# One list for five engines: an in-kernel planner fixes every engine's order in a fused SSM-convolution and MLP block, with loads off the ScalarE queue and smaller evictions

## The chip, the cores and the metric

The kernel runs on one core of a Trainium2 chip. The core has five engines that each work through their own list of instructions in order and wait for one another by semaphores: TensorE (PE in the profile, with its weight loads as PEld), VectorE (DVE), ScalarE (ACT), GpSimd (POOL) and SyncE (SP, which here only issues DMAs). ACT and POOL can issue DMAs too. Matrix products land in PSUM, eight banks that are used here as a ring of four tiles of two banks each; a tile comes free when ACT or DVE has copied it out ("evicted" it) to SBUF.

The metric is the device time of one execution in microseconds (us). Before the change its median is 469.66 us over three runs (469.36 to 471.55).

## What is computed

The reference, cut to what matters (B = 1, S = 2048 tokens, D = 640, F = 1728, all bf16):

```python
def _A_ref(q, k, v, shift_k, ssm_k, ssm_D):
    k_shift = sum(k_pad[:, t:t + S, :] * shift_k[:, ks - 1 - t] for t in range(4))
    kv = k_shift * v
    kv_f = rfft2(pad(kv), axes=(1, 2))
    kf_f = rfft2(pad(ssm_k), axes=(1, 2)).transpose(1, 2, 0)
    y = irfft2(kv_f * kf_f)[:S].astype(bfloat16)
    return q * (y + kv * ssm_D)
def _B_ref(x, w1, w2, w3, w4):
    h = gelu(layernorm(x) @ w1)
    g0, g1, g2, g3 = (h quarter by quarter, shifted by +1, -1, +2, -2 tokens)
    x1 = x + concatenate([g0, g1, g2, g3]) @ w2
    return x1 + gelu(layernorm(x1) @ w3) @ w4
sa, ca, ga, sb, cb, gb = (silu(c) @ w_mod).reshape(6, 640)
h = layernorm(A_q) * (1 + ca) + sa
x = A_q + ga * _A_ref(h, A_k, A_v, A_shift_k, A_ssm_k, A_ssm_D)
h = layernorm(x) * (1 + cb) + sb
return x + gb * _B_ref(h, B_w1, B_w2, B_w3, B_w4)
```

So there are two halves: a long convolution over the tokens (done by Fourier transforms that are written as matrix products), and a token-shift MLP.

## The kernel before

**Tables.** The Fourier matrices are built on the chip: POOL makes index ramps (iota, L127), DVE turns them into angles (L128 to L131), ACT takes sines (L135, L138) into F1bd (32x32 blocks), Gs in the region RG, and Hs in RH; EA and EB follow on DVE (L169).

**Loads.** ACT's queue issues ssm_k in five pieces (L90), the shift filter (L91) and k in four pieces (L93). SP's queue issues v with a transpose on the way (L95), then everything later: w_mod, x (A_q, L289), the MLP's weights, the transposes inside the MLP, and the output.

**Convolution.** "Slots" are 32x32 block transposes on DVE (L196) that bring time into the partitions. stage1 (L200) multiplies by F1bd, four matmuls to a PSUM tile of 1024 columns; stage2 (L210) multiplies by Gs, three frequencies to a tile, so 960 columns and eleven tiles for each of its two halves. Both run twice: for the kernel ssm_k (result KSX in R3) and for the signal kv (result XS in R5). Between the two come the shift filter (k is transposed on PE, evicted by ACT at L240, multiplied by diagonal matrices at L245, and multiplied by v on DVE at L248) and the six pieces of the modulation (L265). inverse1 (L350) multiplies the spectra on DVE (L358, L359; the second factor KSY is KSX with its halves swapped by DMA, in two buffers), and multiplies by EA and EB on PE; its evictions are all ACT's. inverse2 (L377) ends the convolution for two or three token tiles at a time. Evictions alternate between ACT and DVE by the patterns "AD" and "AAD" (make_evac, L181).

**MLP.** It runs in eight groups g of 256 tokens (two tiles A of 128): make_q (L328, layernorm of A_q, with 1-column steps on POOL for each tile), chain_a, chain_b, chain_c (residual, second layernorm, third layernorm; each with a square sum on ACT at L322 and a six-step finish on POOL, L313 to L318), a DMA transpose (L431), w1 (L439, L443), gelu on ACT, w2 (L492), another layernorm and DMA transpose (L501, L502), w3 (L513), gelu, w4 (L527), three DVE steps (L532 to L534) and the output DMA. The loop at L545 interleaves group g's chains and w1 with w2 of g-1 and w3, w4 of g-2.

**What sets the order.** The code is written stage by stage, and the framework's scheduler puts each engine's instructions into an order of its own when the program is built. DMAs of one queue are issued in order.

**Names that the prediction uses.** stage1, stage2, inverse1, inverse2 and the MLP's w1 to w4 as above; T01 holds stage1's result, later inverse1's, later the weights w3 and w4; Rb holds w_mod, later the products of inverse1, later y; "x" is A_q in Ra.

Of the kernel before, what the change touches and what calls it, by code (L numbers as in the profile page):

```python
# [16 lines left out]
P = 128  # L17
# [8 lines left out]

@with_exitstack
def kernel(
# [14 lines left out]
    psA = ctx.enter_context(tc.tile_pool(name="psA", bufs=4, space=PSUM))  # L43

# [5 lines left out]
    R5 = mem.tile([P, 20640], BF, name="R5")  # L50
    RG = mem.tile([P, 8192], BF, name="RG")
    RH = mem.tile([P, 4096], BF, name="RH")
    RK = mem.tile([P, 2048], BF, name="RK")
# [5 lines left out]
    ident = mem.tile([P, P], BF, name="ident")  # L59
    cga, sga, cb1, sbv, gbv = (modv[:, j, :] for j in range(5))  # L60
    T0, T1 = T01[:, 0:10240], T01[:, 10240:20480]
# [7 lines left out]
    vT = R5[:, 10400:20640].rearrange("p (b n) -> p b n", b=ND)  # L69
# [10 lines left out]
    KSY = [Rb[:, 8192:10240], RK[:]]  # L80
    y_all = Rb[:].rearrange("p (a d) -> p a d", d=D)

# [4 lines left out]
    with nc.allow_non_contiguous_dma(reason="tiny"):  # L87
        nc.scalar.dma_start(Dcol[:], A_ssm_D.rearrange("(b p) -> p b", p=P))
    for b in range(ND):
        nc.scalar.dma_start(sT[:, b, :], A_ssm_k[b * P:(b + 1) * P, :])  # L90
    nc.scalar.dma_start(skT[:], A_shift_k.rearrange("(b p) j -> p b j", p=P))  # L91
    for sc in range(4):
        nc.scalar.dma_start(ktok[:, 4 * sc:4 * sc + 4, :], k_flat[512 * sc:512 * sc + 512, :].rearrange("(t p) d -> p t d", p=P))  # L93
    for sc in range(4):
        nc.sync.dma_start_transpose(vT[:, :, sc * 512:(sc + 1) * 512], v_flat[sc * 512:(sc + 1) * 512, :])  # L95
    with nc.allow_non_contiguous_dma(reason="tiny"):
        nc.sync.dma_start(c_col[:], c.rearrange("o (b p) -> p (o b)", p=P))


    make_identity(nc, ident[:])  # L100
    mhalf = mem.tile([P, 4], F32, name="mhalf")
    nc.vector.memset(mhalf[:], -0.5)
    pidx = mem.tile([P, 1], I32, name="pidx")
    nc.gpsimd.iota(pidx[:], pattern=[[0, 1]], base=0, channel_multiplier=1)
    b_pos = mem.tile([P, 1], F32, name="b_pos")
    b_neg = mem.tile([P, 1], F32, name="b_neg")
    nc.vector.memset(b_pos[:], PI_LO)
    nc.vector.memset(b_neg[:], -PI_LO)
    T1i = T1.bitcast(I32)
    T1f = T1.bitcast(F32)  # L110
    ang_no = [0]

    def pcol(modulus, mult, add):
        ti = small.tile([P, 1], I32, name="pcol_i", tag="pcol_i")
        nc.vector.tensor_single_scalar(ti[:], pidx[:], modulus - 1, ALU.bitwise_and)
        tf = small.tile([P, 1], F32, name="pcol_f", tag="pcol_f", bufs=4)
        if mult != 1 or add != 0:
            nc.vector.tensor_scalar(tf[:], ti[:], float(mult), float(add), ALU.mult, ALU.add)
        else:
            nc.vector.tensor_copy(tf[:], ti[:])  # L120
        return tf

    def angles(s_col, n, pattern, base, q):
        o = 1536 * (ang_no[0] % 3)
        ang_no[0] += 1
        ti, ms, ma = (T1i[:, o + 512 * i:o + 512 * i + n] for i in range(3))
        nc.gpsimd.iota(ti, pattern=pattern, base=base, channel_multiplier=0)  # L127
        nc.vector.tensor_scalar(ms, ti, s_col, None, ALU.mult)  # L128
        nc.vector.tensor_single_scalar(ms, ms, q - 1, ALU.bitwise_and)
        nc.vector.tensor_scalar(ma, ti, s_col, float(q // 4), ALU.mult, ALU.add)  # L130
        nc.vector.tensor_single_scalar(ma, ma, q - 1, ALU.bitwise_and)  # L131
        return ms, ma

    def sin_to(dst, ms, q):
        nc.scalar.activation(dst, ms, ACT.Sin, scale=-2.0 * PI_LO / q, bias=b_pos[dst.start_partition():dst.start_partition() + dst.shape[0], :])  # L135

    def nsin_to(dst, ms, q):
        nc.scalar.activation(dst, ms, ACT.Sin, scale=2.0 * PI_LO / q, bias=b_neg[dst.start_partition():dst.start_partition() + dst.shape[0], :])  # L138

    cos_to = sin_to  # L140

    s32 = pcol(32, 1, 0)
    s32o = pcol(32, 2, 1)
    s64 = pcol(64, 1, 0)
    nc.gpsimd.memset(F1bd[:], 0.0)
    ms, ma = angles(s32[:], 32, [[2, 32]], 1, 128)
    for q in range(4):
        sl = slice(32 * q, 32 * q + 32)
        cos_to(F1bd[sl, q, 0, :], ma[sl, :], 128)
        nsin_to(F1bd[sl, q, 1, :], ms[sl, :], 128)  # L150
    for kb in range(4):
        ms, ma = angles(s64[:], 512, [[2, 8], [128, 64]], 1 + 16 * kb, 8192)
        k2s = slice(8 * kb, 8 * kb + 8)
        ms3, ma3 = (t.rearrange("p (a b) -> p a b", a=8) for t in (ms, ma))
        cos_to(Gs[:, k2s, 0, 0, :], ma3, 8192)
        nsin_to(Gs[:, k2s, 0, 1, :], ms3, 8192)
        sin_to(Gs[:, k2s, 1, 0, :], ms3, 8192)
        nc.gpsimd.tensor_copy(Gs[:, k2s, 1, 1, :], Gs[:, k2s, 0, 0, :])
    nc.gpsimd.affine_select(out=RQ[:, 0:2560].rearrange("p (a m) -> p a m", m=P),
# [7 lines left out]
    for E, i, src, sg in ((EA, 0, cs, (sc_, -sc_)), (EA, 1, sn, (sc_, -sc_)), (EB, 0, sn, (-sc_, -sc_)), (EB, 1, cs, (sc_, sc_))):  # L167
        for o in range(2):
            nc.vector.tensor_scalar_mul(E[64 * o:64 * o + 64, i, :], src[64 * o:64 * o + 64, :], sg[o])  # L169
# [58 lines left out]
    for b in range(ND):  # L228
        for h in range(2):
            stage1(sL, b, h, ev)  # L230
# [368 lines left out]
```

## Time and profile before

| what | value |
|---|---|
| median of three runs | 469.66 us |
| profiled execution | 471.74 us |
| its span, first to last instruction | 470.0 us |
| busy: PE, DVE, ACT, POOL | 308.2, 251.3, 228.6, 81.8 us |
| instructions | 7694 |
| mean granted TensorE clock | 0.855 |
| DMA traffic | 35.07 MB |

The profiled execution lies 2.08 us above the median, and 1.74 us of it are outside the span. No engine is busy all the time: PE has the most work, 66% of the span. A view by stretches gives each engine's busy time between two moments; a row of the timeline begins with its start and its duration; a row of the groups ends with "busy, mean ns of one | idle time before it, and what ended it".

### The profile page before, as it was taken

What the parts mean: (1) busy time and instruction counts of PE and PEld (TensorE: products, weight loads), DVE (VectorE), ACT (ScalarE), POOL (GpSimd) and SP (SyncE); (2) the same over time, 40 slices, a digit from 0 to 9 for tenths busy, and PEclk for the clock granted to TensorE, in tenths of its full rate; (3) what the DMA queues carried; (4) which work ended last, traced back from release to release, by engine and by line L of the source; (5) the groups of instructions that cost most, each with busy time, mean ns of one, the idle gap of its engine ahead of it and who ended that gap; (6) DMA issues with size and microseconds to landing.
All of it is one profiled execution on the core that took longest, in us unless ns stands there. A gap on an engine that the chain in (4) does not pass through costs nothing. (4 is left out here: it accounts for less than half of the span.)

```text
span 470.0 us, 7694 instructions
## 1 busy us (share of the span) xinstructions
PE 308.2 (66%) x3089; PEld 223.8 (48%) x3092; DVE 251.3 (53%) x441; ACT 228.6 (49%) x326; POOL 81.8 (17%) x238
## 2 busy tenths in 40 slices
PE   0031887676876508632720497996969889799995
PEld 0021643464556407521510374764747566477773
DVE  4967743984697779577777616133241522314113
ACT  0098724674499626664554271452716436251430
POOL 1331000000000250044544221120211202111000
PEclk9995899959997758965775599898979989899998
DMA  8950700014358507301671111012130111211211
GB/s 244 268 158 1 211 0 1 0 46 141 116 108 195 152 3 178 91 4 28 145 263 29 28 29 40 18 28 57 29 57 11 34 42 29 56 29 28 30 29 29
DMA packets 51219, 35.07 MB, mean 75 GB/s; under 512 B 35632, under 2 KB 48624, under 8 KB 51184
## 3 DMA queue, kind: packets, MB, share of 16 engines
q1 hardware_dynamic: 47040, 29.34, 26.4%
q10 hardware_dynamic: 4144, 5.25, 3.6%
q8 instruction: 24, 0.39, 0.3%
q14 instruction: 11, 0.09, 0.1%
HBM read 18.85 MB, written 2.62 MB: 46 GB/s over the span
## 5 line engine op out<-in xcount | busy, mean ns | idle before, releaser
L527 PE MATMUL ps_w<-T,R 128*128 128x320 bf16 x448 | 69.0, 300 | 0.8 <-ACT R L515 0.6
L439 PE MATMUL ps_w<-R,RG 128*128 128x256 bf16 x160 | 31.8, 386 | 56.2 <-DMA R<-RK 56.2
L513 PE MATMUL ps_w<-R,T 128*128 128x256 bf16 (+1 forms) x560 | 64.4, 273 | 0.0
L513 PEld LDWEIGHTS <-T 128*128 128x128 bf16 (+1 forms) x560 | 54.5, 99 | 8.2 <-issue 1.7
L527 PEld LDWEIGHTS <-R 128*128 128x128 bf16 x448 | 40.6, 97 | 29.0 <-issue 7.5
L439 PEld LDWEIGHTS <-RG 128*128 128x128 bf16 x160 | 21.1, 135 | 65.3 <-issue 55.3
L188 ACT CAST R<-ps_s 128x960 bf16<-128x960 f32 (+1 forms) x30 | 42.5, 1590 | 9.4 <-PE ps_s L218 9.4
L322 ACT ACTIVATE RG<-R 128x640 bf16<-128x640 bf16 x32 | 23.6, 736 | 45.7 <-DVE R L495 22.9
L207 PE MATMUL ps_s<-F1bd,Rb 128*128 128x256 bf16 x80 | 13.6, 342 | 41.7 <-ACT F1bd L138 27.4
L218 PE MATMUL ps_s<-T,RG 64*128 64x160 bf16 x512 | 28.9, 274 | 15.7 <-ACT R L188 7.3
L495 DVE SCALAR_TENSOR_TENSOR R<-ps_w,R 128x640 bf16<-128x640 f32 x16 | 13.1, 824 | 42.9 <-PE ps_w L492 42.8
L366 PE MATMUL ps_i<-EB,Rb 128*128 128x128 bf16 x160 | 22.2, 242 | 19.8 <-DVE Rb L359 19.8
L218 PEld LDWEIGHTS <-RG 64*128 64x128 bf16 x512 | 24.8, 114 | 19.9 <-issue 19.8
L532 DVE TENSOR_TENSOR T<-ps_w,R 128x640 bf16<-128x640 f32 x16 | 13.1, 820 | 39.4 <-PE ps_w L527 39.4
L440 ACT ACTIVATE R<-ps_w 128x1024 bf16<-128x1024 f32 x8 | 8.2, 1022 | 52.8 <-PE ps_w L439 52.8
L336 POOL TENSOR_SCALAR ln_rs<-ln_mv 128x1 f32<-128x1 f32 x16 | 4.7, 298 | 163.5 <-DVE ln_mv L333 143.7
L421 DVE TENSOR_SCALAR R<-Ra,ln_rs,ln_nb 128x640 bf16<-128x640 bf16 x16 | 6.4, 445 | 48.0 <-POOL ln_nb L318 48.0
L207 PEld LDWEIGHTS <-Rb 128*128 128x128 bf16 x80 | 9.6, 121 | 45.4 <-issue 42.4
L515 ACT ACTIVATE R<-ps_w 128x1024 bf16<-128x1024 f32 x24 | 23.6, 1021 | 12.6 <-PE ps_w L513 12.4
L340 ACT ACTIVATE RQ<-Ra,ln_nb,ln_rs 128x640 bf16<-128x640 bf16 x16 | 14.5, 918 | 29.2 <-POOL ln_nb L338 28.2
L492 PE MATMUL ps_w<-RG,R 128*128 128x320 bf16 x160 | 25.4, 301 | 3.8 <-ACT R L440 1.7
L366 PEld LDWEIGHTS <-Rb 128*128 128x128 bf16 x160 | 17.1, 110 | 21.2 <-DVE Rb L359 21.0
(110 smaller groups left out, 594.2 us busy)
## 6 DMA issues: line engine op xcount, KB each, us to landing
Rb<-in_w_mod_dram SPq DMA_DIRECT2D x6, 800.0 KB, 4.7
Ra<-in_A_ssm_k_dram ACTq DMA_DIRECT2D x5, 512.0 KB, 7.1
R<-in_A_k_dram ACTq DMA_DIRECT2D x4, 640.0 KB, 7.9
RK<-R SPq DMA_DIRECT2D x10, 256.0 KB, 3.7
Rb<-R SPq DMA_DIRECT2D x10, 256.0 KB, 3.5
Ra<-in_A_q_dram SPq DMA_DIRECT2D x4, 640.0 KB, 10.6
out_dram<-RH SPq DMA_DIRECT2D x64, 40.0 KB, 1.6
T<-in_B_w_dram SPq DMA_DIRECT2D x1, 2160.0 KB, 9.5
```

Source lines behind the costliest of these rows:

```text
L188: nc.scalar.copy(dst, src)
L207: nc.tensor.matmul(psv[:, ml, :], lhsT=xL[:, s0:s0 + P], rhs=F1r, start=True, stop=True)
L218: nc.tensor.matmul(psv[:, g, kl, :], lhsT=Gs[64 * g:64 * g + 64, k0 + kl, cc, :, :].rearrange("p o n -> p (o n)"), rhs=T1h[h][64 * g:64 * ...
L322: nc.scalar.activation(junk, src, ACT.Square, scale=float(D) ** -0.5, accum_out=stat[:, li, 1, t:t + 1])
L340: nc.scalar.activation(qt, xt, ACT.Identity, scale=rs[:], bias=nb[:])
L366: nc.tensor.matmul(psv[:, w, :], lhsT=TB[:, o:o + P], rhs=EBf, start=False, stop=True)
L439: nc.tensor.matmul(ps[:, fb, :], lhsT=w1_sb[:, b, 160 * fb:160 * fb + P], rhs=hT[:, b, :], start=(b == 0), stop=(b == ND - 1))
L492: nc.tensor.matmul(ps[:, hf, 0:320], lhsT=gsf[:, fb, c0:c0 + P], rhs=w2_sb[:, fb, 320 * hf:320 * hf + 320], start=(fb == 0), stop=(fb == 4))
L495: nc.vector.scalar_tensor_tensor(hv, ps[:, :, 0:320], 1.0, hv, ALU.mult, ALU.add, accum_out=stat[:, 2, 0, 2 * g + i:2 * g + i + 1])
L513: nc.tensor.matmul(ps[:fw, fl, :], lhsT=w3_sb[:, b, fb * P:fb * P + fw], rhs=xT[:, b, :], start=(b == 0), stop=(b == ND - 1))
L515: nc.scalar.activation(g3[g % 2][:, f0:f0 + fn, :], ps[:, 0:fn, :], ACT.Gelu_apprx_tanh)
L527: nc.tensor.matmul(ps[:, hf, 0:320], lhsT=g3[g % 2][:fw, fb, i * P:(i + 1) * P], rhs=w4_sb[:fw, fb, 320 * hf:320 * hf + 320], start=(fb == ...
```

## The change

The kernel's statements are wrapped into tasks. Each task has an engine (or a choice between ACT and DVE), an assumed cost, what it reads and writes, a priority, and the PSUM tile that it takes or frees. A planner inside the kernel (Planner.run) places them one after the other on five imagined clocks and sorts them by their planned start; they are then emitted in that order under manual_schedule, which leaves each engine's order as written. The planner runs while the program is built; the chip sees only the order.

What else is different:

- ssm_k pieces 0 and 1 go to SP's queue, pieces 2 to 4, the shift filter and k to POOL's queue. ACT issues no DMA.
- Angles: one ramp serves four tables, its offset is added on DVE by a column (gcol, hcol). The copies on POOL (L158) become four more sines on ACT.
- stage2 takes two frequencies to a tile: 640 columns, 16 tiles for each half, instead of 960 and eleven. Which engine evicts is the planner's choice, for the second half of the signal it is ACT's alone.
- The shift filter goes pair of feature blocks by pair of feature blocks ("b-major") over all tokens, in twelve units, interleaved with stage2 of the kernel. So the block transposes (slots) of kv can begin when a pair of blocks is done.
- KSY has three buffers instead of two.
- The layernorm of A_q: statistics of 16 tiles into one array, its finish on POOL for 6, 4 and 6 tiles at a time.
- All six pieces of inverse2 stand ahead of the first w1, with all evictions on ACT; the loads of w3 and w4 follow them on SP's queue.
- chain_c has four buffers instead of three.

```diff
+class Planner:
+    def run(self):
+        ...
+        while todo:
+            best = None
+            for e in engs:
+                cand = None
+                for t in ready[e]:
+                    ...
+                    st = max(rt, free[e])
+                    k = (st, t.prio) if st > free[e] else (free[e], t.prio)
+                    ...
+                if cand is not None and (best is None or cand[2] < best[2]):
+                    best = (cand[0], cand[1], cand[2], e)
+            ...
+        order.sort(key=lambda t: (t.start, t.no))
+        return order
...
     for b in range(ND):
-        nc.scalar.dma_start(sT[:, b, :], A_ssm_k[b * P:(b + 1) * P, :])
+        add("SP" if b < 2 else "POOL", 1.5 if b < 2 else 1.0, lambda e, b=b: (nc.sync if b < 2 else nc.gpsimd).dma_start(sT[:, b, :], ...),
...
-        nc.scalar.dma_start(ktok[:, 4 * sc:4 * sc + 4, :], ...)
+        add("POOL", 1.0, lambda e, sc=sc: nc.gpsimd.dma_start(ktok[:, 4 * sc:4 * sc + 4, :], ...),
...
-    def stage2(XSd, h, evac):
-        for k0 in range(0, 32, 3):
-            kn = min(3, 32 - k0)
+    def stage2(XSd, dreg, h, prio0, step=0.0, eng=("ACT", "DVE")):
+        for k0 in range(0, 32, 2):
...
+    units = [(sc, bp) for bp in ((0, 1), (2, 3), (4,)) for sc in range(4)]
...
+    for j in range(12):
+        k_transpose(j, 20 + (j - 2) / 3.0)
+    for j in range(12):
+        k_shift(j, 20 + j / 3.0)
     for h in range(2):
-        stage2(KSX, h, ev)
+        stage2(KSX, "R3", h, 20 + 2 * h, 1.0 / 16)
...
     for h in range(2):
-        stage2(XS, h, ev)
+        stage2(XS, "R5", h, 50, eng="ACT" if h else ("ACT", "DVE"))
...
+    for A in range(6):
+        ln1_stats(A, 66)
+    ln1_fin(0, 6, 66)
     for h in range(2):
         for b in range(ND):
-            inverse1(h, b, ev)
-            if h == 1:
-                make_q(b)
+            inverse1(h, b, 55 if h == 0 else 57)
+    for A in range(5):
+        make_q(A, 67)
...
+    for i, tl in enumerate(rest):
+        inverse2(tl, 105 + 5 * i)
...
+    dma("SP", 2200, w3t[0], w=[("T01", 0, ND * F)], prio=101)
+    dma("SP", 2200, w3t[1], w=[("T01", 10240, 10240 + NF * D, "w4")], prio=101)
...
+    order = pl.run()
...
+    with tc.manual_schedule():
+        for t in order:
+            t.fn(t.on)
```

Three places show what the order becomes.

ACT, the start of the program, before (the loads of ssm_k, of the filter and of k, then the first sines):

```order
L88 DMA Dcol<-in_A_ssm_D_dram 128x5x1
L90 DMA Ra<-in_A_ssm_k_dram 128x2048 x5
L91 DMA skT<-in_A_shift_k_dram 128x5x4
L93 DMA R_67<-in_A_k_dram 128x4x640 x4
L135 ACT_TABLE_LOAD
L135 ACTIVATE F1bd<-T_66,b_pos 32x32
```

ACT, the same place with the change:

```order
L331 ACT_TABLE_LOAD
L331 ACTIVATE F1bd<-R_67,b_neg 32x32 x2
L331 ACTIVATE F1bd<-R_67,b_pos 32x32 x3
L331 ACTIVATE F1bd<-R_67,b_neg 32x32
L331 ACTIVATE F1bd<-R_67,b_pos 32x32
```

The eleven DMA issues are gone from ACT, and the first sine stands at the head of its list.

DVE, where the signal's stage2 ends and inverse1 begins, before (L190 are evictions of stage2, L358 and L359 the products of inverse1, L332 and L333 the layernorm statistics of x):

```order
L190 CAST R_68<-ps_s_1249 128x320x3
L358 TENSOR_TENSOR Rb<-R_68,R_67 128x4x16x32
L359 TENSOR_TENSOR Rb<-R_68,RK 128x4x16x32
L190 CAST R_68<-ps_s_1291 128x320x3
L190 CAST R_68<-ps_s_1333 128x320x3
L358 TENSOR_TENSOR Rb<-R_68,R_67 128x4x16x32 x2
L332 BN_STATS ln_st<-Ra 128x6 x3
L333 BN_AGGR ln_mv<-ln_st 128x2
```

DVE, the same place with the change (L569 and L570 are the statistics, of which the last of eight tiles is shown, L520 to L524 the last pieces of the modulation, L608 and L610 the products, L588 and L589 the finish of a q tile):

```order
L569 BN_STATS ln_st<-Ra 128x6 x2
L570 BN_AGGR mv_93<-ln_st 128x2
L520 TENSOR_SCALAR modv<-ps_mod 128x640
L608 TENSOR_TENSOR Rb<-R_68,R_67 128x4x16x32
L522 CAST modv<-ps_mod 128x640
L524 CAST modv<-ps_mod 128x640
L608 TENSOR_TENSOR Rb<-R_68,R_67 128x4x16x32
L610 TENSOR_TENSOR Rb<-R_68,RK 128x4x16x32
L588 TENSOR_TENSOR RQ<-RQ,modv 128x640
L589 TENSOR_TENSOR RQ<-RQ,modv 128x640
L610 TENSOR_TENSOR Rb<-R_68,Rb 128x4x16x32
```

The statistics of eight tiles of x now stand ahead of the first product; before, four first products and two second ones stood ahead of them, and the other fourteen products behind.

SP, around the first transposes of the MLP, before (L354 and L355 are the swaps KSY, L431 the transposes after chain_c, L551 to L553 the loads of w3 and w4, L502 the transposes ahead of w3):

```order
L354 DMA RK<-R_67 64x2048
L355 DMA RK<-R_67 64x2048
L431 DMA_TRANSPOSE R_67<-RK 128x5x128 x4
L553 DMA T_66<-in_B_w_dram 64x640
L551 DMA T_66<-in_B_w_dram 128x5x1728
L552 DMA T_66<-in_B_w_dram 128x13x640
L502 DMA_TRANSPOSE R_67<-RH 128x5x128 x2
```

SP, the same place with the change (L603 the swaps, L900 to L902 w3 and w4, L734 the transposes after chain_c, L839 those ahead of w3):

```order
L603 DMA Rb<-R_67 64x2048 x2
L900 DMA T_66<-in_B_w_dram 128x5x1728
L901 DMA T_66<-in_B_w_dram 128x13x640
L902 DMA T_66<-in_B_w_dram 64x640
L734 DMA_TRANSPOSE R_67<-RK 128x5x128 x6
L839 DMA_TRANSPOSE R_67<-RH 128x5x128 x2
```

The two large loads moved from behind the transposes of the first two groups to ahead of them.

More of the change, by code (lines that the diff above doesn't have):

```diff
@@ L43 @@
     psA = ctx.enter_context(tc.tile_pool(name="psA", bufs=4, space=PSUM))
+    pl = Planner(4)
+    add = pl.add
+    eng_of = {"ACT": nc.scalar, "DVE": nc.vector}
     Ra = mem.tile([P, 10240], BF, name="Ra")
@@ L111 @@
[L111 to L146, printed above, removed]
+    stat = mem.tile([P, 3, 2, NT], F32, name="stat")
@@ L267 @@
[L267 to L280 removed]
+        ps = Slot()
```

937 lines of the change are left out of this document (623 added, 314 removed).

## The prediction, made before the changed kernel ran

> **What bounds the kernel now.** I read the view by stretches first, cut where the stages change. Columns: the stretch and its length, then busy time of PE, PEld, DVE, ACT and POOL with the number of instructions, the granted clock, DMA share and GB/s.
>
> ```profile
> 0.00:27.40 27.40, 0.00 (x0) 0.01 (x1) 16.23 (x34) 3.49 (x10) 6.35 (x15) 1.00 1.03 266
> 27.40:55.10 27.70, 13.37 (x80) 9.63 (x81) 24.01 (x46) 23.64 (x34) 5.80 (x8) 0.69 0.28 78
> 55.10:109.30 54.20, 37.40 (x417) 25.58 (x418) 34.28 (x26) 29.49 (x23) 0.00 (x0) 0.87 0.10 27
> 109.30:133.30 24.00, 19.79 (x140) 13.65 (x139) 15.20 (x16) 11.11 (x12) 0.00 (x0) 0.93 0.40 125
> 133.30:153.70 20.40, 13.85 (x257) 11.77 (x256) 16.79 (x13) 20.10 (x15) 0.00 (x0) 0.82 0.87 192
> 153.70:200.00 46.30, 24.14 (x399) 22.50 (x401) 34.21 (x59) 25.53 (x28) 10.64 (x32) 0.78 0.39 100
> 200.00:220.70 20.70, 4.42 (x295) 2.91 (x281) 15.76 (x35) 11.55 (x20) 9.65 (x24) 0.60 0.09 18
> 220.70:411.10 190.40, 142.04 (x1120) 99.20 (x1121) 80.79 (x194) 86.47 (x163) 45.96 (x147) 0.85 0.24 55
> 411.10:470.00 58.90, 53.19 (x409) 38.60 (x409) 14.07 (x26) 17.24 (x27) 3.40 (x12) 0.98 0.16 29
> ```
>
> The rows are: loading; tables and stage1 of the kernel (with the row above, A); shift filter and its stage2 (B); modulation and stage1 of the signal (C); its stage2 (D); inverse1 (E); inverse2 up to the first w1 (F); the MLP (G, two rows). Only the fifth (ACT 20.10 of 20.40) and the last are filled by one engine. In the others the busiest engine has 65 to 90% of the time: they are bound by waiting in line, and that is what an order can change. The chain that ended last runs through the last row on PE alone:
>
> ```profile
> 404.85 3.64 PE ps_w L439 x20
> 411.06 1.80 PE ps_w L492 x12
> 428.95 2.82 PE ps_w L492 x20
> 431.78 7.76 PE ps_w L513 x70
> 439.54 8.45 PE ps_w L527 x56
> 464.33 0.83 DVE T L532
> ```
>
> **Stage A.** ACT's queue holds the cause:
>
> ```profile
> 1.24 11.06 ACTq L90 DMA_DIRECT2D Ra<-in_A_ssm_k_dram  x5
> 12.99 10.75 ACTq L93 DMA_DIRECT2D R<-in_A_k_dram  x4
> 23.84 1.28 ACT L135 ACT_TABLE_LOAD   x1 [23.84 <-issue]
> 44.16 3.95 ACT L188 CAST T<-ps_s 128x1024 bf16<-128x1024 f32 x4
> ...
> L135 ACT ACTIVATE RG<-T,b_pos 128x512 bf16<-128x512 int32 x8 | 5.4, 709 | 0.0
> L196 DVE STREAM_TRANSPOSE Rb<-Ra 128x1024 int32<-128x1024 int32 x5 | 9.9, 1989 | 0.1
> L188 ACT CAST T<-ps_s 128x1024 bf16<-128x1024 f32 x20 | 19.3, 1013 | 14.7 <-PE ps_s L207 14.5
> L190 DVE CAST T<-ps_s 128x1024 bf16<-128x1024 f32 x20 | 23.3, 1219 | 2.4 <-PE ps_s L207 2.0 <-ACT RH L135 0.4
> ```
>
> Nine issues keep ACT from its first sine until 23.84, and all sines come before its first eviction at 44.16. With the change ACT starts when DVE has the first angles, about 3 us; eight small sines bring it to 5, sixteen of 0.71 (four of them POOL's copies before) to 16, then 13 evictions of 1.01 to 29.5. DVE had 16.2 + 24.0 busy in the first two rows of the stretches; less five slots (9.9) and ten evictions (12.2) 18 us are left for the angles, 32 long steps and small ones, so some 0.5 a step. Now it makes sixteen of them (8 us), five slots of 1.99 (to 20) and seven evictions of 1.22: 29. The sines for RH move into B. The loads are no later than that: ssm_k, k and v are 7.9 MB, at the first row's 266 GB/s 30 us. **A ends at 30 instead of 55.1.**
>
> A loading price that this trace cannot show is POOL's: no DMA was issued there. Nearest rows: ACT spent 21.8 us on nine issues under a full DMA (share 1.03). If POOL's first load left at 3 us instead of 1.2, nothing changes; if its k pieces land 8 us later (POOL beginning only after DVE's angles), B waits those 8. I take nothing and keep 8 as an end. The Trainium skill, page "DMA: Bandwidth & Descriptors", section "SWDGE vs HWDGE vs iDMA", says that POOL writes such descriptors itself and is locked out of SBUF while DVE runs certain fast modes; no run here shows it, and by it the 8 us would be paid. The same page, section "Issuing engines are not separate DMA queues", says that issuing from several engines saves only the issue time, usually small beside the transfer. Here the row speaks otherwise, since the issue time itself was 21.8 us of ACT; by the rule A would gain a few us only.
>
> **Stage B.** Rows for the evictions:
>
> ```profile
> L188 ACT CAST R<-ps_s 128x960 bf16<-128x960 f32 x26 | 40.3, 1712 | 9.4 <-PE ps_s L218 9.4
> L188 ACT CAST R<-ps_s 128x640 bf16<-128x640 f32 x4 | 3.2, 791 | 0.0
> L190 DVE CAST R<-ps_s 128x960 bf16<-128x960 f32 x14 | 24.5, 1778 | 4.9 <-PE ps_s L218 4.9
> ```
>
> The last tile of each half already had 640 columns, two frequencies: 0.79 on ACT, while 960 cost 1.55 to 1.78. Both stage2 together cost 40.3 + 3.2 + 24.5 = 68.0; 64 tiles at 0.79 cost 50.6. Half of it, B's share, falls from 34 to 25.3. Into B come eight sines (5.7), the silu (1.5) and 16 angle steps, EA, EB and a copy (some 10). ACT and DVE had 29.5 + 34.3 = 63.8 busy here; now 63.8 - 8.7 + 17.2 = 72.3, by free choice 36.2 each, beside PE's 37.4. Packed perfectly, B takes 37; packed as before (37.4 of 54.2) it takes 54. With transposes, filter and stage2 alternating on PE the wait of one is covered by the next, so I take the middle, 44. **B ends at 74.**
>
> **Stage C.** Three of six modulation pieces stay beside stage1; PE's 19.8 loses half of the row
>
> ```profile
> L265 PE MATMUL ps_mod<-Rb,silu_bc 128*128 128x320 bf16 x60 | 10.2, 327 | 4.0 <-DMA Rb<-in_w_mod_dram 3.4 <-ACT R L188 0.5
> ```
>
> and is 14.7; the evictions are twelve on ACT (12.2) and eight on DVE with three small ones (12.2). The rest of the old 24 was waiting for w_mod, whose buffer is now free early. **C ends at 88.**
>
> **Stages D and E.** Stage2 of the signal has 24 evictions on ACT: 19 us, to 107. But DVE's order now has eight tiles of statistics ahead of the first product, and they need x. Its loads may start only when stage1 has read Ra:
>
> ```profile
> 133.41 3.07 SPq L289 DMA_DIRECT2D Ra<-in_A_q_dram  x4
> DMA to landing us min/median/max: 6.5/10.6/14.4
> ...
> L332 DVE BATCH_NORM_STATS2 ln_st<-Ra 128x6 f32<-128x320 bf16 x32 | 14.0, 470 | 0.0
> 193.76 1.22 DVE L358 TENSOR_TENSOR Rb<-R,R 128x2048 bf16<-128x2048 bf16 x1
> 194.90 1.22 DVE L359 TENSOR_TENSOR Rb<-R,RK 128x2048 bf16<-128x2048 bf16 x1
> 199.98 0.69 ACT L188 CAST Rb<-ps_i 128x640 bf16<-128x640 f32 x1 [0.82 <-PE ps_i L385]
> ```
>
> The last of the four landed some 16.5 us after the first issue, so x is there at 104.5, eight tiles of 2 x 0.47 end at 112, and the first product starts at 112.8, six us behind stage2's end. That is the price of this order; free of it E would begin at 107. From there DVE is the bound: 20 products, 1.14 apart in the two rows, 22.8; five q finishes of two steps over 640 columns, 4.2 (0.42 a step, an estimate from 1.22 for 2048); two copies of 640, 1.6 at the eviction's 0.79; one for swaps that come late: 29.6, to 142.4. Before, products and statistics waited for one another and took 46.3. From the last product's end (196.1) to the first eviction of inverse2 took 3.9. **So inverse2's first eviction is at 146 instead of 199.98.**
>
> **Stage F.** From there to the first w1 took 20.7. The chain of evictions, residual, two layernorms stays, and DVE now does two groups in turn. But w3 and w4 stand ahead of the transposes on SP's queue:
>
> ```profile
> T<-in_B_w_dram SPq DMA_DIRECT2D x1, 2160.0 KB, 9.5
> T<-in_B_w_dram SPq DMA_DIRECT2D x1, 2080.0 KB, 14.6
> R<-RK SPq DMA_TRANSPOSE x16, 2.6
> ```
>
> Issued 0.6 us apart, the one landed after 9.5 and the other after 14.6: the queue serves them one after the other. They may start when inverse2 has read T01, about 11 us in (twelve evictions, all ACT's: four of 640 columns at 0.69, eight of 960 at 1.03 in proportion), and are done at 26; transposes issued at 17 come after that, at 28. **First w1 at 174 (before 220.66).** If the transposes are not held up, 7 us less.
>
> **Stage G.** PE must do 8 x (w3 + w4 16.2 + w2 2.8 + w1). w1 took 3.64 on a PE that had idled, 20 matmuls; w3's pace, 7.76 for 70, gives 2.2, and with its fifth block 2.8. The first w3 cannot come before two rounds w1 to w2 (6.2 by the chain, and w1 again), w2, and the way from w2 to w3, with a gelu of the third w1 ahead of it in ACT's order. That way is long:
>
> ```profile
> 271.45 1.80 PE L492 MATMUL ps_w<-RG,R 128*128 128x320 bf16 x12 [0.18 <-ACT R L446]
> 277.79 2.53 SPq L502 DMA_TRANSPOSE R<-RH  x2
> ```
>
> w2 ended at 273.25, the second transpose left at 279.1 and landed 2.6 later: 8.5. In all 26 us, in which three w1 and two w2 are done. Behind it 8 x 16.2 + 6 x 2.8 + 5 x 2.8 = 160.4. DVE and ACT have half of that. I add 7 for waits that a fixed order does not foresee, and the end 5.7 (464.31 to 470.0). 26 + 160.4 + 7 + 5.7 = 199: **span 373.** Before, this took 249, with PE busy 142 of the 190 in its first stretch; w1 waited for its transposes (us in total, times, longest):
>
> ```profile
> PE ps_w L439 <- DMA R<-RK: 56.2, 8, 24.8
> ```
>
> The profiled execution is 1.74 longer than its span, so 375; the median lay 2.1 lower: I say 373.
>
> **The rivals.**
> - POOL's loads land late: +8, 381. For it: eight issues on an engine whose issue price is unknown. Against: 30 us of room. 0.13.
> - B packs no better than before: 54 instead of 44, 383. For it: the ring of four tiles is unchanged. 0.14.
> - w3 and w4 do not hold up the transposes: 366. Against: the two landings. 0.14.
> - Every later group of the MLP still waits for its transposes as before, 4.5 us a group without the longest ((56.2 - 24.8) / 7), for five groups: 396. For it: the transposes have the same length; against: chains now run several groups ahead. 0.12.
> - The smaller evictions do not do what they should, costing 0.79 only when they follow a long one, else two thirds of 1.6, 1.06: 0.27 x 24 in D and half as much in B, 383. 0.08.
> - Loading off ACT gains little (the issuing rule as a mechanism: DVE's angles wait for POOL, which issues first): A ends at 50, 393. 0.04. This is the rule of the Trainium skill, "DMA: Bandwidth & Descriptors", that issuing elsewhere saves little; the 23.84 row speaks against it.
> - Slower: PE's fixed order in the MLP sets up to five other groups' work between a group's w1 and w4, so one late transpose holds all. The longest wait of before was 24.8. A group has 21.8 of PE's work, so from 15 us of waiting in every group on (8 x 37 + 174 = 470) the kernel is slower; with 24.8 in each the span is 547. Against: seven of the eight waits were far shorter. 0.02.
>
> **How the numbers follow.** The forecast has 0.33. The range reaches down to 355 (transposes early, B at 39, fewer waits) and up to 398 (a little over the dearest of the likely rivals); left out are the slow case and sums of rivals. Half a per cent is about what a measurement of this kernel tells from no change; only the slow rival comes near it: faster 0.97, same 0.01, slower 0.02.
>
> **What would show it.** ACT's first activation at 3 instead of 25; first eviction near 16; kv's stage1 near 74; 640-column evictions at 0.79; first product of inverse1 right behind the statistics and these behind x's landing; the first L734 transposes landing behind w4; then PE without gaps over 1 us. Wrong if k lands after 35, if PE waits within B for evictions, or if PE idles for transposes after the first w3.

## The result, and the profile after

| | before | after |
|---|---|---|
| median | 470.61 us (4 runs, 469.36 to 471.55) | 369.47 us (4 runs, 368.48 to 370.18) |
| ratio | 1 | 0.785, 95% interval 0.782 to 0.788 |
| span of the profiled execution | 470.0 us | 367.2 us |
| busy: PE, DVE, ACT, POOL | 308.2, 251.3, 228.6, 81.8 us | 290.1, 234.7, 226.8, 80.1 us |
| mean granted TensorE clock | 0.855 | 0.916 |

The changed kernel takes 369.5 us; forecast were 373, between 355 and 398. The trace of one experiment, that with the loads back on ACT, comes from a disturbed execution (a span of 752.6 us) and is not used; its time is the median of its three other runs.

The view by stretches of the changed kernel, cut where the stages change, with the columns as before:

```profile
0.00:32.20 32.20, 13.29 (x80) 9.51 (x81) 29.52 (x53) 24.89 (x38) 10.95 (x22) 0.95 0.96 244
32.20:72.80 40.60, 35.67 (x420) 21.73 (x427) 37.24 (x54) 32.28 (x48) 0.00 (x0) 1.00 0.30 88
72.80:85.60 12.80, 12.43 (x104) 9.67 (x103) 11.79 (x12) 10.15 (x11) 0.00 (x0) 1.00 0.64 193
85.60:110.70 25.10, 16.80 (x287) 12.22 (x286) 14.99 (x35) 16.40 (x27) 2.83 (x5) 0.93 0.84 192
110.70:145.20 34.50, 24.59 (x396) 22.96 (x400) 32.69 (x45) 23.61 (x26) 2.16 (x13) 0.80 0.43 108
145.20:173.00 27.80, 7.01 (x456) 5.36 (x442) 25.07 (x64) 22.74 (x39) 16.69 (x35) 0.56 0.60 181
173.00:361.40 188.40, 180.28 (x1368) 132.32 (x1368) 81.55 (x177) 96.78 (x178) 47.53 (x126) 0.97 0.20 39
361.40:367.20 5.80, 0.02 (x1) 0.00 (x0) 1.81 (x3) 0.00 (x0) 0.00 (x0) 0.67 0.13 34
```

Now almost every stretch has an engine that fills it: DVE 29.5 of 32.2 in A, 37.2 of 40.6 in B, 32.7 of 34.5 in E and 25.1 of 27.8 in F; PE 12.4 of 12.8 in C and 180.3 of 188.4 in the MLP. Only in D (85.6 to 110.7) the sums hide it, because two engines take turns. ACT evicts stage2 without a pause until 101.9; DVE waits 9.73 us for x, which lands at 102.0, and then has eight tiles of statistics ahead of the first product (timelines of ACT and DVE; in brackets, how long the engine stood idle before, and for what):

```profile
86.87 15.03 ACT L229 CAST R<-ps_s 128x640 bf16<-128x640 f32 x24
101.99 0.89 DVE L569 BATCH_NORM_STATS2 ln_st<-Ra 128x6 f32<-128x320 bf16 x2 [9.73 <-DMA Ra<-in_A_q_dram]
110.67 1.22 DVE L608 TENSOR_TENSOR Rb<-R,R 128x2048 bf16<-128x2048 bf16 x1
```

The cuts against the forecast:

| end of | before | forecast | measured |
|---|---|---|---|
| A: first transpose of k on PE | 55.1 | 30 | 32.2 |
| B: first stage1 of kv | 109.3 | 74 | 72.8 |
| C: first stage2 of the signal | 133.3 | 88 | 85.6 |
| D: first product of inverse1 | 153.7 (stage2's end) | 112.8 | 110.7 |
| E: first eviction of inverse2 | 199.98 | 146 | 145.2 |
| F: first w1 | 220.66 | 174 | 173.0 |
| first w3 | 271.0 | 200 | 199.3 |
| span | 470.0 | 373 | 367.2 |

ACT's first table and first eviction, from the timeline of the changed kernel (start, duration, what):

```profile
2.82 1.28 ACT L331 ACT_TABLE_LOAD   x1 [2.82 <-DVE R L323]
16.36 5.54 ACT L229 CAST T<-ps_s 128x1024 bf16<-128x1024 f32 x6
```

The groups of stage2's evictions in the changed kernel (busy and mean ns of one, then idle time ahead):

```profile
L229 ACT CAST R<-ps_s 128x640 bf16<-128x640 f32 x49 | 31.4, 744 | 3.2 <-PE ps_s L418 3.2
L231 DVE CAST R<-ps_s 128x640 bf16<-128x640 f32 x15 | 11.7, 816 | 0.1
```

The wait of w1 for its transposes, from the changed kernel's list of waits (total, times, longest):

```profile
PE ps_w L764 <- DMA R<-RK: 16.3, 1, 16.3
```

The end of its chain of waits (start, duration, what):

```profile
347.29 5.68 PE ps_w L854 x50
352.97 8.46 PE ps_w L877 x56
361.45 0.84 DVE T L883
```

ACT begins at 2.82 instead of 23.84 and evicts at 16.36 instead of 44.16. Both stage2 cost 43.1 us of eviction, before 68.0. w1 waits for its transposes once, at the start, instead of eight times (56.2 us). From the first w3 at 199.3 to 361.4 PE has no gap.

### The profile page after: what moved, and what is told of

Read it like the earlier page. It is cut to its first block, busy times and chain, and to the rows that moved or that the text cites. A ratio compares the mean times of both kernels' runs of the same rounds, so it can differ in the third digit from the quotient of the medians.

```text
span 367.2 us, 7656 instructions
## 1 busy us (share of the span) xinstructions
PE 290.1 (79%) x3086; PEld 213.8 (58%) x3092; DVE 234.7 (64%) x436; ACT 226.8 (62%) x362; POOL 80.1 (22%) x201
## 4 chain that ended last, share of the span: by engine, by line
PE 55%; DVE 25%; DMA 8%; ACT 4%; issue 3%; POOL 3%; SPq 1%; DVEq 0%; POOLq 0%; ACTq 0%
PE ps_w L877 18%; PE ps_w L854 18%; PE ps_w L819 6%; PE ps_w L764 5%; DMA Ra<-in_A_q_dram 4%; DVE ln_st L569 3%; DVE Rb L386 3%; DVE R L480 2%; DVE Rb L610 2%; DVE Ra L386 2%; ACT T L229 2%; PE ps_ksh L474 2%; DMA R<-RK 2%; PE ps_s L399 2%; DVE T L231 2%
## 5 line engine op out<-in xcount | busy, mean ns | idle before, releaser
L859 ACT ACTIVATE R<-ps_w 128x1024 bf16<-128x1024 f32 x24 | 24.5, 1022 | 61.7 <-PE ps_w L854 61.6
L877 PEld LDWEIGHTS <-R 128*128 128x128 bf16 x448 | 41.7, 97 | 25.6 <-issue 8.4
L229 ACT CAST R<-ps_s 128x640 bf16<-128x640 f32 x49 | 31.4, 744 | 3.2 <-PE ps_s L418 3.2
L764 PE MATMUL ps_w<-R,RG 128*128 128x256 bf16 x160 | 20.4, 287 | 16.3 <-DMA R<-RK 16.3
L619 PE MATMUL ps_i<-EA,Rb 128*128 128x128 bf16 x160 | 23.2, 243 | 11.4 <-DVE Rb L608 11.4
L229 ACT CAST T<-ps_s 128x1024 bf16<-128x1024 f32 x25 | 23.7, 1020 | 7.3 <-PE ps_s L399 7.3
L764 PEld LDWEIGHTS <-RG 128*128 128x128 bf16 x160 | 16.4, 103 | 19.7 <-issue 16.6
L229 ACT CAST T<-ps_i 128x1024 bf16<-128x1024 f32 x20 | 19.6, 1014 | 10.1 <-PE ps_i L620 6.5
L619 PEld LDWEIGHTS <-Rb 128*128 128x128 bf16 x160 | 17.8, 111 | 11.9 <-DVE Rb L608 11.9
L418 PEld LDWEIGHTS <-RG 64*128 64x128 bf16 x512 | 18.1, 94 | 10.9 <-issue 10.2
L819 PEld LDWEIGHTS <-R 128*128 128x128 bf16 x160 | 15.9, 103 | 13.6 <-ACT R L780 4.8
L399 PEld LDWEIGHTS <-Rb 128*128 128x128 bf16 x80 | 9.5, 120 | 22.2 <-DVE Ra L442 14.3
L620 PEld LDWEIGHTS <-Rb 128*128 128x128 bf16 x160 | 17.6, 111 | 5.0 <-DVE Rb L610 5.0
```

Of the source, the lines that this page charges most:

```text
L229: nc.scalar.copy(dst, src(ps.tile))
L399: nc.tensor.matmul(psv[:, ml, :], lhsT=xL[:, s0:s0 + P], rhs=F1r, start=True, stop=True)
L418: nc.tensor.matmul(psv[:, g, kl, :], lhsT=Gs[64 * g:64 * g + 64, k0 + kl, cc, :, :].rearrange("p o n -> p (o n)"), rhs=T1h[h][64 * g:64 * ...
L619: nc.tensor.matmul(psv[:, w, :], lhsT=TA[:, o:o + P], rhs=EAf, start=True, stop=False)
L620: nc.tensor.matmul(psv[:, w, :], lhsT=TB[:, o:o + P], rhs=EBf, start=False, stop=True)
L764: nc.tensor.matmul(pt[:, fb, :], lhsT=w1_sb[:, b, 160 * fb:160 * fb + P], rhs=hT[:, b, :], start=(b == 0), stop=(b == ND - 1))
```

## The experiments

All are timed in three rounds beside the kernel before; a time below is the median, to be read against 369.5 (runs from 368.5 to 370.2), or against 470 for kernels made from the one before.

### The same statements in the scheduler's order

```diff
-    with tc.manual_schedule():
-        for t in order:
-            t.fn(t.on)
+    for t in pl.tasks:
+        t.fn(t.on)
```

The statements are emitted in the order of the code, and the framework's scheduler orders each engine as it did before. Which engine evicts what stays the planner's choice.

> The changed kernel's statements, all of them, but put in order by the framework's scheduler as before, not by the planner's list. Theory (the order itself carries most of the gain, above all in the MLP): the first w3 and the waits of w1 for transposes come back; of the 101 us gained 45 to 75 are lost, so 415 to 445 us. Rival (loads, smaller evictions, the filter's loop and inverse2 ahead of the MLP carry it): under 385 us.

Measured: 459.2 us, ratio to before 0.979 (0.975 to 0.983). More is lost than the theory said: of the 101 us the edits give only some 11 in the scheduler's order, and the other 90 come with the order. Two lines of this kernel's list of waits:

```profile
PE ps_w L764 <- DMA R<-RK: 53.0, 8, 17.5
PE ps_s L399 <- ACT F1bd L331: 35.3, 1, 35.3
```

Its view by stretches, cut at A's end, the end of C, the start of inverse2, the first w1 and the first w3:

```profile
0.00:62.70 62.70, 14.68 (x80) 10.08 (x81) 37.14 (x80) 30.52 (x48) 10.64 (x22) 1.00 0.54 152
62.70:130.80 68.10, 57.36 (x554) 37.67 (x556) 42.44 (x41) 34.05 (x48) 0.00 (x0) 0.92 0.25 73
130.80:187.90 57.10, 34.31 (x577) 29.72 (x577) 48.09 (x87) 39.87 (x51) 8.17 (x21) 0.88 0.60 140
187.90:210.40 22.50, 9.06 (x512) 5.70 (x512) 18.34 (x47) 20.07 (x32) 8.34 (x21) 0.58 0.13 24
210.40:258.80 48.40, 19.56 (x103) 12.95 (x104) 22.47 (x58) 19.07 (x37) 9.68 (x31) 0.63 0.35 110
258.80:457.10 198.30, 173.53 (x1267) 122.93 (x1264) 58.95 (x126) 79.72 (x149) 29.25 (x108) 0.94 0.16 34
```

Against the changed kernel A is 30.5 us longer (62.7 to 32.2), B and C 14.7, first w1 to first w3 22.1 (48.4 to 26.3) and the rest 30.4 (198.3 to 167.9); D to F together are 7.8 shorter (79.6 to 87.4). PE's first matmul waited 35.3 us for ACT's first tables. So the loads, smaller evictions and the filter's loop are all there, and A is even longer than the 55.1 of before. The next two runs show why. The runs after them take other pieces of the 90 us apart, not all of it.

### Only the loads, in the kernel before

```diff
-        nc.scalar.dma_start(Dcol[:], ...)
+        nc.sync.dma_start(Dcol[:], ...)
...
-        nc.scalar.dma_start(sT[:, b, :], ...)
+        (nc.sync if b < 2 else nc.gpsimd).dma_start(sT[:, b, :], ...)
-    nc.scalar.dma_start(skT[:], ...)
+    nc.gpsimd.dma_start(skT[:], ...)
-        nc.scalar.dma_start(ktok[:, 4 * sc:4 * sc + 4, :], ...)
+        nc.gpsimd.dma_start(ktok[:, 4 * sc:4 * sc + 4, :], ...)
```

> The kernel before with only its loads moved (two pieces of ssm_k to SP, three pieces, the filter and k to POOL); framework's order. Theory (ACT's issue time sets stage A): ACT starts near 3, then DVE's 40 us of work in the first two stages becomes the limit, stage A ends at 38 to 42 instead of 55.1 and the whole shifts by 13 to 18: 452 to 458 us. Rival (rule): within 3 us of 470.

Measured: 476.9 us, ratio 1.017 (1.013 to 1.021): a little slower, near 2%, with every run above all those of the kernel before. Theory and rival both missed. The timeline of ACT in this kernel:

```profile
0.79 1.28 ACT L177 ACT_TABLE_LOAD   x1 [0.79 <-PEq L583]
30.58 0.21 ACT L177 ACTIVATE silu_c<-c_col 128x5 f32<-128x5 bf16 x1 [28.50 <-DMA c_col<-in_c_dram]
32.61 0.98 ACT L138 ACTIVATE F1bd<-T,b_neg 32x32 bf16<-32x32 int32 x3 [1.83 <-DVE T L129]
```

And that of DVE:

```profile
30.82 0.82 DVE L178 CAST silu_bc<-silu_c 128x640 bf16<-128x640 f32 x1 [12.81 <-ACT silu_c L177]
```

With ACT's list empty the scheduler put the silu of c at its head. Its 1.2 KB come over SP, behind v's four transposes, at 30.6; ACT stands in front of the sines until then, and so does DVE, for 12.81 us, where the next step of the silu stands ahead of the angles. The kernel of the first run has the same wait: its silu is at 30.2, its first sine at 32.6.

### The same, with the load of c first

```diff
+        nc.sync.dma_start(c_col[:], c.rearrange("o (b p) -> p (o b)", p=P))
     for sc in range(4):
         nc.sync.dma_start_transpose(vT[:, :, sc * 512:(sc + 1) * 512], ...)
-        nc.sync.dma_start(c_col[:], c.rearrange("o (b p) -> p (o b)", p=P))
```

> The kernel before with the loads off ACT as in the earlier run, and the 1 KB load of c ahead of v's transposes on SP. Theory (in that run ACT and DVE stood still for the silu of c, whose load waited behind v until 30): DVE begins its angles right behind the fifth slot, at 18 instead of 31, all later stages 11 to 13 us earlier than in that run: 463 to 467 us. Rival (issuing on POOL itself slows stage A): 474 or more.

Measured: 467.2 us (10 runs), ratio 0.995 (0.992 to 0.997); 9.7 us less than without this line, just past the upper edge of what the theory said. So the wait was the cause of the loss. Even issued ahead of v at 2.3, c is there only at 17, so DVE begins its angles at 20.4 where the theory had 18; the timeline of ACT in this kernel:

```profile
17.36 0.21 ACT L177 ACTIVATE silu_c<-c_col 128x5 f32<-128x5 bf16 x1 [15.28 <-DMA c_col<-in_c_dram]
```

So moving the loads, with c first, gives 3 us in the scheduler's order, where the forecast counted 25 for stage A: that sum presupposed ACT's and DVE's order of the changed kernel. How much of the first run's loss this wait makes was not tried there.

### The loads back on ACT, in the changed kernel

```diff
-        add("SP" if b < 2 else "POOL", ..., (nc.sync if b < 2 else nc.gpsimd).dma_start(sT[:, b, :], ...)
+        add("ACT", 2.2, ... nc.scalar.dma_start(sT[:, b, :], ...), prio=-5)
-        add("POOL", 1.0, ... nc.gpsimd.dma_start(ktok[...], ...)
+        add("ACT", 2.7, ... nc.scalar.dma_start(ktok[...], ...), prio=-5)
```

The filter goes with them.

> The changed kernel with ssm_k, the filter and k issued on ScalarE's queue again, ahead of its first sine, the planner knowing of it. Theory (ACT's issue time sets stage A): first sine near 23 instead of 4, stage1 of ssm_k ends near 50 instead of 32, all later stages shift with it: 385 to 390 us. Rival (the rule that other issuing engines save only the issue time, little beside the transfer): under 373 us.

Measured: 386.1 us, 16.7 more; the theory's size. No trace that can be used shows where the time went; that ACT's issues hold the first sine, as in the kernel before, is inferred from the size. In the planned order the loads on ACT cost 17, in the scheduler's order taking them away gives 3. The Trainium skill, page "DMA: Bandwidth & Descriptors", section "Issuing engines are not separate DMA queues", says that issuing on several engines saves only the time to initiate the DMA, which is usually small. In the planned order it was not small: 17 us.

### Stage2 in tiles of 960 columns again

```diff
-        for k0 in range(0, 32, 2):
+        for k0 in range(0, 32, 3):
+            kn = min(3, 32 - k0)
```

> The changed kernel with stage2 in tiles of three frequencies (960 columns, eleven per half) as before. Theory (960 columns cost 1.55 to 1.78 us where 640 cost 0.74 to 0.82): evictions of both stage2 rise by 20 to 25 us over two engines; half of B's share shows, the signal's is partly hidden behind the landing of x: 375 to 381 us. Rival (an eviction costs by its columns, about 1.15 for 960): within 2 us of 369.5.

Measured: 374.9 us, 5.4 more, the lower end of the theory. The groups of evictions in this kernel:

```profile
L229 ACT CAST R<-ps_s 128x960 bf16<-128x960 f32 x33 | 52.0, 1733 | 2.3 <-PE ps_s L419 2.3
L231 DVE CAST R<-ps_s 128x960 bf16<-128x960 f32 x7 | 11.9, 1787 | 0.2 <-PE ps_s L419 0.2
L229 ACT CAST R<-ps_s 128x640 bf16<-128x640 f32 x4 | 3.1, 786 | 0.0
L229 ACT CAST Rb<-ps_i 128x960 bf16<-128x960 f32 x8 | 7.4, 957 | 0.0
```

67.0 us instead of 43.1, so 24 us of busy time more, of which 5.4 are seen: the first stage1 of kv comes at 78.3 instead of 72.8. The signal's half adds next to nothing to that: the first product is at 116.4 instead of 110.7, 5.7 later. But it is no longer x and the statistics that it waits for. ACT evicts stage2 until 116.1, and DVE waits for a modulation piece that stands behind stage2 on PE:

```profile
115.65 0.82 DVE L521 TENSOR_SCALAR modv<-ps_mod 128x640 bf16<-128x640 f32 x1 [2.12 <-PE ps_mod L508]
```

So the slack that x had left is used up. The price is not one of size: inverse2's tiles of 960 columns, in another layout, take 0.96.

### The filter by tokens again

```diff
-    units = [(sc, bp) for bp in ((0, 1), (2, 3), (4,)) for sc in range(4)]
+    units = [(sc, bp) for sc in range(4) for bp in ((0, 1), (2, 3), (4,))]
```

What a unit waits for in the transposed k is adapted to it.

> The changed kernel with the shift filter's twelve units ordered token quarter by token quarter, as before, instead of pair of feature blocks by pair. Theory (only the new loop lets the five slots of kv, 1.95 us each on DVE, run while the filter still goes on): the slots come behind the filter's end, stage B is 4 to 9 us longer: 373.5 to 378.5 us. Rival (DVE does evictions in that time instead and the sum is the same): within 1.5 us of 369.5.

Measured: 370.7 us (369.2 to 371.0), not to be told from 369.5: the rival. The slots do move, and begin at 65.4 instead of 49.7, but DVE evicts in their place before and PE's list goes on; the first stage1 of kv is even at 70.9, before 72.8. This part of the change is worth nothing measurable here.

### Shorter lead of the chains

```diff
     def chain_a(g, prio):
-            add("DVE", 0.42, ..., prio=prio)
+            add("DVE", 0.42, ..., prio=prio, after=w4_of.get(g - 3, []))
...
+            w4_of[g] = [t0]
```

The planner may place the chain of group g only behind the start of w4 of g-3; the instructions are the same.

> The changed kernel with the chain of group g planned only behind the start of w4 of group g-3, so less far ahead of PE; the same instructions. Theory (the chains' lead is what removed the waits of w1 for its transposes): 3 to 5 us of PE waiting come back in each of five groups: 385 to 398 us. Rival (PE has enough other work in any case): 368 to 373.

Measured: 406.1 us, 36.6 more, beyond the theory's range. From this kernel's list of waits:

```profile
PE ps_w L766 <- DMA R<-RK: 26.5, 6, 16.1
PE ps_w L856 <- DMA R<-RH: 16.3, 2, 10.7
PE ps_w L821 <- ACT R L768: 4.8, 5, 2.4
PE ps_w L821 <- ACT R L782: 4.6, 5, 1.6
```

Less the longest, the one ahead of the first w1 that the changed kernel has too, 26.5 - 16.1 = 10 us of waiting come back for w1, 16.3 for w3 (2.6 in the changed kernel) and 9.4 for w2 behind gelu (5.5 in the changed kernel); and PE's busy time rises from 290.1 to 299.5 us. Together that is some 37 us, about the whole loss. The lead is what makes the MLP dense, and of the parts of the order that were tried it is the largest.

### w3 and w4 behind the first transposes

```diff
-    dma("SP", 2200, w3t[0], w=[("T01", 0, ND * F)], prio=101)
...
         chain_c(g, rb, pr)
+        if g == 1:
+            tr = [pl.tasks[-1], pl.tasks[-3]]
+            ... add("SP", 0.55, lambda e, fn=fn: fn(nc.sync), ..., after=tr)
```

> The changed kernel with the loads of w3 and w4 behind the transposes of the first two groups on SP's queue; nothing else moves but the place of a few evictions' names. Theory (the queue serves in order, so 4.2 MB stood ahead of the transposes): the first transposes land 2.6 to 3.1 after their issue instead of 6.4, first w1 at 169.5 instead of 173.0; the first w3 moves less, 0 to 3.5 us, because the second layernorm's chain and the third w1 stand between: 366 to 369.5. Rival (transposes are slow there by themselves, or not held up): first w1 stays at 173, no change. Rival (w3 itself comes late): slower by the time that PE waits for it, first w3 after 199.3.

Measured: 365.1 us (364.4 to 367.1), 4.4 less than the changed kernel and a little more than the theory said; all its runs lie below all of that one's. The first w1 is at 168.4 instead of 173.0. Of these 4.6 us 3.8 lie between the first eviction of inverse2 and w1, where the transposes land after 2.67 instead of 6.43; 0.8 were there before. It is the fastest version by its median, though the run with both edits below (366.0) can't be told from it.

### The same loads on another queue

```diff
-    w3t = [lambda q: q.dma_start(w3_sb, ...), lambda q: q.dma_start(w4_sb...
+    w3t = [lambda q: nc.gpsimd.dma_start(w3_sb, ...), lambda q: nc.gpsimd.dma_start(w4_sb...
```

Nothing else moves on PE, ACT, DVE or SP; on POOL the three issues stand among layernorm steps.

> The changed kernel with the same order on PE, ACT and DVE, but w3 and w4 issued on POOL's queue instead of SP's, at the same planned moment, so both are under way when the first transposes are issued. Theory (order within one queue held the transposes): they land 2.6 to 3.1 after their issue instead of 6.4, first w1 at 169 to 170.5, 365 to 369 us, as with the loads behind them. Rival (the 16 DMA engines are full, whichever queue): landing stays over 5, first w1 at 172 or later, 369 us or more.

Measured: 370.7 us (369.3 to 371.8). The rival's time, but not by its landing: the second transpose leaves 3.5 us later than in the changed kernel and then takes 3.80. Of the 3.5 us 1.1 are there at the first residual, before the loads are issued; the rest comes while the three issues stand in the chain's way on POOL. The last run shows it more cleanly.

### Statistics later

```diff
-    for A in range(6, NT):
-        ln1_stats(A, 122 + 10 * (A - 6) // 2)
-        if A in (9, 15):
-            ln1_fin(...)
...
         chain_c(g, rb, pr)
+        if g in (0, 1):
+            tr2 = [pl.tasks[-2], pl.tasks[-4]]
+            for A in range(*((6, 10), (10, 16))[g]):
+                ln1_stats(A, pr + 12, tr2)
+            ln1_fin(...)
```

> The changed kernel with the statistics of tiles 6 to 15 and their finish placed behind the first two groups' transposes instead of ahead of the first residual. Theory (seven tiles on DVE and a finish on POOL stand in the first chain's way): the first residual starts right behind the first eviction of inverse2, near 144 instead of 148.25, and the first transposes are issued 4 to 8 us earlier; but w3 and w4 stand ahead of them on SP's queue, so first w1 only 2 to 4 us earlier: 365.5 to 367.5 us. Rival (the statistics only move and are missed later): 368.5 to 372.

Measured: 373.8 us, 4.3 more, in neither range. The first w1 is at 172.6, only 0.4 earlier, held by the loads; and the third group's w1 now waits for its transposes, behind the moved statistics; the timeline of PE in this kernel:

```profile
195.90 4.42 PE L764 MATMUL ps_w<-R,RG 128*128 128x256 bf16 x20 [5.34 <-DMA R<-RK]
```

That w1 stood at 188.56 in the changed kernel, without a wait.

> The late statistics and w3, w4 behind the first two groups' transposes together. Theory (the two stand in one another's shadow: each hides part of the other): first w1 at 160 to 166 instead of 173, more than the sum of the single gains, 357 to 362 us. Rival (the next limit, ACT's and POOL's steps between w1 and w2, takes it): 363 to 366.

With w3 and w4 behind the transposes as well: 366.0 us, the rival's range. First w1 is at 162.3, six earlier than with the loads moved alone, but from there to the end it takes 201.5 us (span 363.8), there 194.3 (362.7): the third group's w1 waits 7.7 us for its transposes. The ten tiles of statistics that were moved cost DVE about 1 us each wherever they stand in this stretch; what moves is the place of the wait.

### Fewer statistics moved, loads on the other queue

```diff
+        if g in (1, 2):
+            for A in range(*{1: (8, 12), 2: (12, 16)}[g]):
+                ln1_stats(A, pr + 12, tr2)
-           lambda q: q.dma_start(w4_sb...
+           lambda q: nc.gpsimd.dma_start(w4_sb...
```

The statistics of tiles 6 and 7 join those of the first six ahead of inverse1.

> The load on the other queue, and only the statistics of tiles 8 to 15 moved, behind the transposes of groups 1 and 2. Theory (in the earlier runs ten statistics delayed the third group's transposes, and the loads stood ahead of them): first w1 at 160 to 166, no wait over 3 us of the third w1: 357 to 362 us. Rival (the chain from w1 over gelu, w2 and its layernorm to the first w3 is the next limit): 363 to 367 us.

Measured: 375.3 us, 5.9 more; theory and rival both missed. The first w1 is 1.3 later than in the changed kernel, and the third group's w1 waits again, on PE's timeline:

```profile
195.63 3.63 PE L764 MATMUL ps_w<-R,RG 128*128 128x256 bf16 x20 [6.77 <-DMA R<-RK]
```

The chain of waits just ahead of the first w1 (start, duration, what), in this kernel:

```profile
163.19 10.94 DMA R<-RK
174.27 1.87 PE ps_w L764 x8
```

In the kernel with the loads on POOL alone:

```profile
169.95 3.80 DMA R<-RK
```

In the changed kernel:

```profile
166.48 6.43 DMA R<-RK
173.01 3.61 PE ps_w L764 x20
```

In the kernel with w3 and w4 behind:

```profile
165.57 2.67 DMA R<-RK
```

The last piece of the load, its issue and its time to landing, in the changed kernel and in the last one:

```profile
158.03 5.77 SPq L902 DMA_DIRECT2D T<-in_B_w_dram  x1
T<-in_B_w_dram SPq DMA_DIRECT2D x1, 80.0 KB, 13.3
161.34 0.61 POOL L902 DMA_DIRECT2D T<-in_B_w_dram  x1
T<-in_B_w_dram POOLq DMA_DIRECT2D x1, 80.0 KB, 12.2
```

It lands at 171.4 and 173.5, in the kernel with the loads on POOL alone at 172.7. Whether the transposes set out at 163.2, 166.5 or 170.0, and whether 4.2 MB were issued before them on POOL's queue or on their own, they land between 172.9 and 174.1, 0.6 to 1.6 us behind that last piece. Without the load they take 2.67. So the queue's order is not needed to hold them: transfers under way do it, on either queue that was tried. By what means the small one stays behind the large one, these runs don't show.

## Why the prediction was right, point by point

- **The total.** The span was forecast at 373 and is 367.2, 5.8 less; the median is only 3.5 off, because the median was taken to lie 2.1 below the profiled execution and lies 0.5 above it. That part is luck. Against the forecast A is 2.2 longer and E 1.3; B is 3.4 shorter, C 1.2 and G 4.9; D and F are within 0.3. So the size holds stage by stage, with small errors that partly cancel.
- **Stage A.** The mechanism held (first eviction forecast near 16, measured 16.36; the end 2 us late, DVE filling it). Put back on ACT the loads cost 17. But it was presented as a gain of the loads alone: with the scheduler's order it is 3, or a loss of 7. What A became shorter belongs to loads and order together, and to the angles, of which DVE was forecast to make 8 us' worth in A instead of 18; that part was not tried by itself. The reading that outside two stretches the busiest engine has 65 to 90% is wrong for the loading: DVE has 59% there, and the DMA share of 1.03 shows what fills it.
- **POOL's price.** Taken as nothing, rightly: its four issues of k took 3.02 us against ACT's 10.75, and the first transpose of k waits for an eviction, not for k (timelines of POOL and PE):

```profile
4.71 3.02 POOL L255 DMA_DIRECT2D R<-in_A_k_dram  x4
32.21 1.50 PE L461 MATMUL ps_kT<-modv,R 128*128 128x128 bf16 x24 [0.21 <-ACT T L229]
```

The locking that the Trainium skill names for such loads (page "DMA: Bandwidth & Descriptors", section "SWDGE vs HWDGE vs iDMA") does not show as a delay here.

- **Stage B.** Middle of the two bounds, 44, which was a choice and no sum; measured 40.6, with DVE at 37.2. Packing was better than assumed. The sign of being wrong that was named, PE waiting within B for evictions, did show, but small: PE idles 4.9 us of B, at most 1.9 at once. Smaller evictions carry 5.4 by the run with 960 columns; the filter's loop carries nothing.
- **Stages C to E.** C 12.8 for 14; x landed at 102.0 for 104.5, eight tiles of statistics behind it, the first product at 110.7 for 112.8; inverse2's first eviction 34.5 after it for 33.2. DVE is the bound, as said. The price of the statistics ahead of the first product was larger than the six us named: stage2's last eviction ends at 101.9, not 107, so the product comes 8.8 us behind it.
- **Stage F.** 27.8 for 28, and the landing of w3 and w4 set it. The mechanism was mis-named: with "the queue serves them one after the other" another queue should have freed the transposes, and it does not. And "7 less if not" was too much: 4.4 by the run, because the chain itself is longer than forecast: the second transpose leaves 21.3 us after inverse2's first eviction, where 17 were taken. Seven statistics stand ahead of the first residual, on DVE's timeline of the changed kernel here:

```profile
148.25 0.44 DVE L707 TENSOR_TENSOR R<-Rb,RQ 128x640 bf16<-128x640 bf16 x1
```

And a finish of six tiles stands ahead of the chain's own step on POOL's:

```profile
159.86 1.60 POOL L576 TENSOR_TENSOR rs<-rs,mhalf 128x6 f32<-128x6 f32 x1
162.89 0.39 POOL L692 TENSOR_TENSOR ln_rs<-stat,ln_m 128x2 f32<-128x2 f32 x1
```

The first residual could have followed the first eviction, which starts at 145.2 and takes 0.7 us, and the chain's step on POOL stood 3.5 us behind the finish. Both are covered by the loads in the changed kernel, so that the stage's total is right although the chain was taken too short.

- **Stage G.** Here is the mis-sized term: 7 us of waits were allowed, and there are none after the first w3; 162.1 of PE work for 160.4, and 5.8 at the end for 5.7. The 26 to the first w3 was 26.3.
- **The rivals.** Waits of 4.5 in each later group did not come, and the run with the shorter lead shows what kept them away. Evictions at 1.06, packing as before and late loads of POOL fell by the rows above. That the transposes are not held up fell too. That loading off ACT gains little fell in the planned order (17 us) and came true in the scheduler's (3). The slower case, PE's fixed order holding everything for one late transpose, did not come; in the kernel with the shorter lead the order did hold PE, up to 10.7 us at once, and it stayed far from 470.

## What to carry to other kernels

Where no engine is full, price the edits within the order that they will run in: freed time goes to what stands next in an engine's list, and a 1 KB load behind a long queue can eat all of it. Give dependent chains a lead of some groups before the dense stage, and keep large loads from starting shortly ahead of a small transfer that the bottleneck waits for; another queue did not help here. Moving statistics within the stretch that DVE fills gained nothing, so look first whether the engine is full there.

## What the runs showed of the hardware that was not expected

- A transpose of 2.67 us takes up to 10.94 with 4.2 MB under way on another engine's queue, and lands as that load ends. The Trainium skill, page "DMA: Bandwidth & Descriptors", section "Issuing engines are not separate DMA queues", says that transfers of all issuers run on the same 16 engines and interleave. The first half agrees; the small one here did not get in between but landed 0.6 to 1.6 us behind the end of the large one.
- Evicting 960 columns took 1.73 us in stage2's layout and 0.96 in inverse2's. Which part of the layout costs it was not tried.
- PE's busy time fell from 308.2 to 290.1 us with the same matmuls: twenty of w1 took 4.42 behind a wait of 5.34 (with the statistics late) and 2.35 in the dense stretch. The mean granted clock rose from 0.855 to 0.916; these runs don't separate the two.

The dense one, on the timeline of PE in the changed kernel:

```profile
207.48 2.35 PE L764 MATMUL ps_w<-R,RG 128*128 128x256 bf16 x20
```
